# Moving both FFN layers ahead of the attention heads, rolling two engines' loops, and storing the output from 128 partitions

## Chip, cores and metric

One core of one Trainium2 chip. The metric is device microseconds (us) of one execution; lower is better. Every kernel was run beside the kernel before on the same chip. The sessions were on different chips, so kernels of different sessions are best compared by their ratios to the kernel before. The time is longer than the "span" of a profile, which goes from the first to the last instruction: about 2.4 us in the kernel before.

## The reference, cut to what matters

One decode step: a layer norm, attention of one query against a cache of 8192 keys for 2 x 32 heads, and a two-layer FFN on the same normalised x; all three are added.

```python
# bf16: x [2,1,512]  k_cache, v_cache [2,32,8192,128]  wq [512,4096]  wo [4096,512]
#       w1 [512,1792]  w2 [1792,512]
xn = _layernorm(x)
q  = (xn @ wq).reshape(B, Sq, H, Dh).transpose(0, 2, 1, 3)
p  = softmax(einsum("bhqd,bhkd->bhqk", q, k_cache) * Dh ** -0.5)
o  = einsum("bhqk,bhkd->bhqd", p, v_cache)
out = x + o.transpose(0, 2, 1, 3).reshape(B, Sq, H * Dh) @ wo \
        + relu(xn @ w1) @ w2
```

K and V are 268.4 MB of the 280.5 MB read. Wq and Wo are 4.19 MB each, W1 and W2 1.835 MB each, and the output is 2 KB.

## The kernel before

All large loads go through one queue, issued by the sync engine, in this order: Wq, then K and V tiles (two head pairs ahead), then W1, W2 and Wo:

```python
nc.sync.dma_start(vs[1][:], A_wq...)
def _(sp):
    load_k(0); load_k(1); load_v(0)
    for t in range(NP - 1):
        if t + R < NP:
            sp.wait_ge(pT, NG * (t + 1))      # the K buffer is free after its transposes
            load_k(t + R)
        sp.wait_ge(sW, t + 1)                 # the V buffer is free after its products
        load_v(t + 1)
    sp.dma_start(x8[:], A_x...)
    sp.dma_start(w1_sb[:], ...); sp.dma_start(w2_sb[:], ...)
    for c in range(3):                        # Wo in rows 0:16, 16:28, 28:32
        sp.dma_start(wo_sb[:, sl, :], wo_v[:, sl, :]).then_inc(dW[2 + c], 16)
    sp.wait_ge(sE, 1)
    sp.dma_start(out.rearrange("b s (c p) -> (b s c) p", p=P), osb[:]).then_inc(dO, 16)
```

For each of 32 head pairs, PE transposes a K tile in 16 groups of 8 (`transposes`), DVE and ACT copy the groups to SBUF (`kcopy`), PE multiplies them with q (`scores`) and then multiplies the previous pair's V tile (`weighted`). DVE and ACT are unrolled over the 32 pairs. The tail, after the last V tile:

```python
# PE
ffn(0, FT // 2); ... ; ffn(FT // 2, FT)       # W1 as weights, 56 matmuls of 2 columns
project(w2_sb, hT, 0, FT, first=True)         # W2 as weights, 56 matmuls
for c in range(3):
    pe.wait_ge(dW[2 + c], 16)
    project(wo_sb, OX, cuts[c], cuts[c + 1])  # lhsT = wo[:, j, c*128:(c+1)*128]
pe.wait_ge(sV, 105)
pe.transpose(tp[1][0:8, 0, :], yT)            # 128 x 8 -> 8 x 128
# DVE
v.tensor_tensor(out=yT[:], in0=ot[0]..., in1=xT..., op=ALU.add)
v.tensor_copy(osb[:], tp[1][0:8, 0, :])       # then the store: 8 rows of 256 B
```

Of the kernel before, what the change touches and what calls it, by code (L numbers as in the profile page):

```python
# [11 lines left out]
R = 2  # L12
# [7 lines left out]
def kernel(  # L20
# [31 lines left out]
    assert KT * H * Dh == SLOT  # L52
    inv_sqrt = float(Dh) ** -0.5
# [10 lines left out]
    def sem(name):  # L64
        return tc.alloc_semaphore(name)
# [4 lines left out]
    wo_sb = sb([P, WJ, D], bf16, "wo_sb")  # L70
    w1_sb = sb([P, KT, Dff], bf16, "w1_sb")
    w2_sb = sb([P, FT, D], bf16, "w2_sb")
    kT = [sb([P, EG, P], bf16, f"kT{i}") for i in range(4)]
    identb = sb([P, P], bf16, "identb")
    sel = sb([H, DQ, P], bf16, "sel")
# [4 lines left out]
    x8 = sb([Bsz * KT, P], bf16, "x8")  # L80
    xT = sb([P, Bsz * KT], f32, "xT")
# [5 lines left out]
    xnT = sb([P, KT, Bsz], bf16, "xnT")  # L87
# [8 lines left out]
    OTf = sb([P, N + 2], f32, "OTf")  # L96
# [4 lines left out]
    hT = sb([P, FT, Bsz], bf16, "hT")  # L101
    yT = sb([P, Bsz, KT], bf16, "yT")
    osb = sb([Bsz * KT, P], bf16, "osb")
# [15 lines left out]
    dX, dX8, dO = sem("dX"), sem("dX8"), sem("dO")  # L119
    dK = [sem(f"dK{i}") for i in range(R)]  # L120
    dV = [sem(f"dV{i}") for i in range(R)]
    dW = [sem(f"dW{i}") for i in range(5)]
    sG, sI, sQ, sQ1 = sem("sG"), sem("sI"), sem("sQ"), sem("sQ1")
    sV, sA, sE = sem("sV"), sem("sA"), sem("sE")
    pT, sS, sT, sB, sW = sem("pT"), sem("sS"), sem("sT"), sem("sB"), sem("sW")
    kR = [sem(f"kR{e}") for e in range(NG)]
    sM, sX, sP, sO = sem("sM"), sem("sX"), sem("sP"), sem("sO")
    sH, sF = sem("sH"), sem("sF")
# [5 lines left out]
    cuts = (0, 16, 28, WJ)  # L134
    qp = ot[1][:, 0:N].rearrange("p (h b) -> p h b", b=Bsz)
# [3 lines left out]
    tpy = tp[2][:].rearrange("p g k -> p (g k)")[:, 0:Bsz * KT]  # L139
    hp = ot[1][:, 0:FT * Bsz].rearrange("p (j b) -> p j b", b=Bsz)  # L140
# [7 lines left out]

    nc.sync.dma_start(vs[1][:], A_wq.rearrange("(p kt) n -> p (kt n)", kt=KT)).then_inc(dV[1], 16)  # L149
    nc.scalar.dma_start(xsb[:], A_x.flatten_outer_dims()).then_inc(dX, 16)  # L150

    block = nc.Block(no_gpsimd_drain=True)
    block.__enter__()

    @block.sync
    def _(sp):
        load_k(0)
        load_k(1)
        load_v(0)
        for t in range(NP - 1):  # L160
            if t + R < NP:
                sp.wait_ge(pT, NG * (t + 1))
                load_k(t + R)
            sp.wait_ge(sW, t + 1)
            load_v(t + 1)
        sp.dma_start(x8[:], A_x.rearrange("b s (c p) -> (b s c) p", p=P)).then_inc(dX8, 16)  # L166
        sp.dma_start(w1_sb[:], B_w1.rearrange("(p kt) f -> p kt f", kt=KT)).then_inc(dW[0], 16)  # L167
        sp.dma_start(w2_sb[:], B_w2.rearrange("(p j) n -> p j n", j=FT)).then_inc(dW[1], 16)  # L168
        for c in range(3):
            sl = slice(cuts[c], cuts[c + 1])  # L170
            sp.dma_start(wo_sb[:, sl, :], wo_v[:, sl, :]).then_inc(dW[2 + c], 16)  # L171
        sp.wait_ge(sE, 1)
        sp.dma_start(
            out.rearrange("b s (c p) -> (b s c) p", p=P), osb[:]
        ).then_inc(dO, 16)


    @block.gpsimd
    def _(g):
# [16 lines left out]
        for u in range(2):  # L196
            g.memset(onesh[u * HP:(u + 1) * HP, u, :], 1.0).then_inc(sI, 1)
            g.wait_ge(sI, 3 + u)
        g.wait_ge(sV, 100)
        for t in range(NP):  # L200
            if t >= R:
                g.wait_ge(sS, t - R + 1)
            g.tensor_copy(q2[t % R][:], qb[:, 2 * t:2 * t + 2]).then_inc(sQ1, 1)  # L203


    @block.tensor
    def _(pe):
# [6 lines left out]
        pe.wait_ge(dV[1], 16)  # L214
        wq_sb = vs[1][:].rearrange("p (kt n) -> p kt n", kt=KT)
        for h in range(H):
            for kt in range(KT):
                i = pe.matmul(  # L218
                    qp[:, h, :],
                    lhsT=wq_sb[:, kt, h * Dh:(h + 1) * Dh],  # L220
                    rhs=xnT[:, kt, :],
                    start=(kt == 0),
                    stop=(kt == KT - 1),
                )
        i.then_inc(sQ, 1)

# [3 lines left out]
        def transposes(r, e):  # L230
            for i in range(EG):
                kk = e * EG + i
                t = pe.transpose(tp[e % 4][:, i, :], ks[r][:, kk * Dh:(kk + 1) * Dh], identb[:])  # L233
            t.then_inc(pT, 1)
# [66 lines left out]
        values(1, NP + 1, 16 * (NP // R + 1))  # L301
        for e in range(NG):
            weighted(1, e)


        w1_v = w1_sb[:].rearrange("p kt (f j) -> p kt j f", j=FT)

        def ffn(j0, j1):
            for j in range(j0, j1):
                for kt in range(KT):  # L310
                    t = pe.matmul(
                        hp[:, j, :],
                        lhsT=w1_v[:, kt, j, :],
                        rhs=xnT[:, kt, :],
                        start=(kt == 0),
                        stop=(kt == KT - 1),
                    )
            return t


        pe.wait_ge(sO, NP + 2)
        pe.wait_ge(sI, 4)
        dbp = Sc[0][:, 0:N].rearrange("p (t u) -> p t u", u=2)
        pe.wait_ge(dX8, 16)
        pe.transpose(tpy, x8[:], identb[0:Bsz * KT, 0:Bsz * KT])
# [3 lines left out]
        pe.wait_ge(dW[0], 16)  # L329
        ffn(0, FT // 2)  # L330

        pe.wait_ge(sV, 102)
# [4 lines left out]
        ffn(FT // 2, FT).then_inc(sF, 1)  # L337
        pe.wait_ge(sV, 103)
# [11 lines left out]

        fin = ot[0][:, 0:KT * Bsz].rearrange("p (b c) -> p c b", c=KT)

        def project(w, act, j0, j1, first=False, last=False):
            for j in range(j0, j1):
                for c in range(KT):
                    t = pe.matmul(  # L356
                        fin[:, c, :],
                        lhsT=w[:, j, c * P:(c + 1) * P],
                        rhs=act[:, j, :],
                        start=(first and j == j0 and c == 0),  # L360
                        stop=(last and j == j1 - 1 and c == KT - 1),
                    )
            return t

        pe.wait_ge(sF, 2)
        pe.wait_ge(dW[1], 16)
        project(w2_sb, hT, 0, FT, first=True)
        pe.wait_ge(sV, 104)
        for c in range(3):
            pe.wait_ge(dW[2 + c], 16)  # L370
            t = project(wo_sb, OX, cuts[c], cuts[c + 1], last=(c == 2))
        t.then_inc(sH, 1)
        pe.wait_ge(sV, 105)
        pe.transpose(
            tp[1][0:Bsz * KT, 0, :], yT[:].rearrange("p b c -> p (b c)"), identb[:]
        ).then_inc(sH, 1)
# [6 lines left out]
    @block.vector  # L383
    def _(v):
        v.memset(eps_t[:], eps).then_inc(sV, 1)
        v.memset(onesb[:], 1.0)
        v.memset(prm[R - 1][:], 0.0).then_inc(sP, 1)
# [17 lines left out]
        v.tensor_copy(xnT[:], tpx).then_inc(sV, 1)  # L405
# [3 lines left out]
            out=qb[:].rearrange("p (b h) -> p b h", b=Bsz),  # L409
            in0=qp.rearrange("p h b -> p b h"),  # L410
            scalar1=inv_sqrt,
            scalar2=None,
            op0=ALU.mult,
        ).then_inc(sV, 94)

        for t in range(NP):
            i = t % R
            for e in range(NG):
                if e not in ON_ACT:
                    v.wait_ge(pT, NG * t + e + 1)  # L420
                    kcopy(v, e)
            v.wait_ge(sS, t + 1)
# [6 lines left out]
            v.wait_ge(sT, t + 1)  # L429
# [4 lines left out]

        v.wait_ge(sH, 1)
        v.tensor_copy(xT[:], tpy)  # L436
        v.reciprocal(out=RD[:], in_=Sc[0][:, 0:N]).then_inc(sV, 1)
        v.wait_ge(sV, 101)
        v.tensor_tensor(
            out=OTn[:].rearrange("p b h -> p (b h)"), in0=OTf[:, 0:N], in1=RD[:], op=ALU.mult  # L440
# [3 lines left out]
        v.wait_ge(sF, 1)  # L444
        v.tensor_scalar(
            out=hT[:], in0=hp, scalar1=0.0, scalar2=None, op0=ALU.max,
        ).then_inc(sF, 1)
# [5 lines left out]
        v.tensor_tensor(  # L453
            out=yT[:],
            in0=ot[0][:, 0:KT * Bsz].rearrange("p (b c) -> p b c", c=KT),
            in1=xT[:].rearrange("p (b c) -> p b c", c=KT),
            op=ALU.add,
        ).then_inc(sV, 1)
        v.wait_ge(sH, 5)
        v.tensor_copy(osb[:], tp[1][0:Bsz * KT, 0, :]).then_inc(sE, 1)  # L460


    @block.scalar
    def _(a):
# [5 lines left out]
        def out_copy(t):  # L470
            c = 2 * t if t >= 0 else N
            a.wait_ge(sW, t + 2)
            a.copy(OTf[:, c:c + 2], ot[t % R][:, 0:2]).then_inc(sO, 1)  # L473

        a.copy(OTf[:, N:N + 1], eps_t[:]).then_inc(sO, 1)
        for t in range(NP):
            i = t % R
            for e in range(NG):
                if e in ON_ACT:
                    a.wait_ge(pT, NG * t + e + 1)  # L480
                    kcopy(a, e)
            a.wait_ge(sB, t + 1)
            a.copy(nm[i][:], bc_of(i)).then_inc(sA, 1)  # L483
            a.wait_ge(sA, t + 2)
            for u in range(2):
# [7 lines left out]
                    accum_out=RS[half, t:t + 1],  # L493
                )
            x.then_inc(sP, 1)
            out_copy(t - 1)
        out_copy(NP - 1)

    block.__exit__(None, None, None)
    nc.sync.wait_ge(dO, 16)  # L500
# [28 lines left out]
```

## Time and profile before

| | before |
|---|---|
| time, median of 6 runs (range) | 662.73 us (662.54 to 662.95) |
| span of the profiled run | 660.4 us |
| PE / DVE / ACT busy | 83% / 38% / 36% |
| read from HBM | 280.50 MB, one queue, 98.9% of the span |
| issue of the store to the end of the span | 660.4 - 657.63 = 2.8 us |

Read it from the transfers: the queue is busy in every slice (90% or more in all but the last, by the page's DMA row), and the landing events of the packed trace come in the order of the issues, 9.7 us apart for most of the 4.19 MB tiles. So an engine's busy share matters only where it delays an issue, or after the last byte. The prediction below shows those lines.

### The profile page before, as it was taken

How to read it: one execution, taken by the hardware profiler on the slowest of the kernel's cores; microseconds unless marked ns; L12 is line 12 of the kernel's file. 1: busy time of each engine (PE TensorE's matmuls, PEld its weight loads, DVE VectorE, ACT ScalarE, POOL GpSimd, SP SyncE). 2: the span in 40 equal slices, each digit the busy share in tenths (PEclk: the TensorE clock that was granted, in tenths of full speed). 3: DMA queues.
4: the chain of work that ended last, by engine and by line, in shares of the span. 5: the costliest groups of instructions: out<-in, count | busy, mean ns of one | idle time of the engine just before them, and what ended most of it. 6: DMA issues, size and time to landing. Idle time of an engine off the chain costs nothing.

```text
span 660.4 us, 26876 instructions
## 1 busy us (share of the span) xinstructions
PE 551.0 (83%) x12864; PEld 537.0 (81%) x12864; DVE 251.4 (38%) x433; ACT 236.7 (36%) x389; POOL 8.5 (1%) x44
## 2 busy tenths in 40 slices
PE   2577999898887889788798987887997878987976
PEld 2577999888887889788798887887987878987875
DVE  1233544344343434434344443343443433443411
ACT  1242444343433334333243343333343333343410
POOL 1000000000000000000000000000000000000000
PEclk9999999998898999889899898899898989997985
DMA  9999999999999999999999999999999999999995
GB/s 381 416 438 429 424 439 427 437 427 431 437 429 437 427 431 433 429 437 429 431 435 427 439 429 431 435 427 439 427 431 433 429 439 425 435 433 429 437 417 246
DMA packets 10133, 280.73 MB, mean 425 GB/s; under 512 B 1154, under 2 KB 1156, under 8 KB 1284
## 3 DMA queue, kind: packets, MB, share of 16 engines
q1 hardware_dynamic: 10112, 280.50, 98.9%
q8 instruction: 10, 0.16, 0.1%
q14 instruction: 7, 0.06, 0.0%
q10 hardware_dynamic: 4, 0.00, 0.0%
HBM read 280.50 MB, written 0.00 MB: 425 GB/s over the span
## 4 chain that ended last, share of the span: by engine, by line
DMA 62%; PE 34%; ACT 1%; issue 1%; SPq 0%; DVE 0%
DMA ks<-in_A_k_cache_dram 56%; PE tp L233 21%; PE Sc L240 10%; DMA wo_sb<-in_A_wo_dram 5%; PE ot L253 3%; ACT kT L380 1%; PE ot L356 0%; PE Sc L288 0%; PE Sc L291 0%; SPq L171 0%; SPq L168 0%; SPq L166 0%; SPq L149 0%; SPq L167 0%; SPq L147 0%
## 5 line engine op out<-in xcount | busy, mean ns | idle before, releaser
L233 PE MATMUL tp<-identb,ks 128*128 128x128 bf16 x4096 | 324.9, 229 | 77.8 <-DMA ks<-in_A_k_cache_dram 75.9
L380 DVE COPY kT<-tp 128x1024 bf16<-128x1024 bf16 x320 | 219.7, 691 | 332.9 <-PE tp L233 332.7
L233 PEld LDWEIGHTS tp<-identb,ks 128*128 128x128 bf16 x4096 | 256.1, 103 | 81.3 <-DMA ks<-in_A_k_cache_dram 79.1
L380 ACT COPY kT<-tp 128x1024 bf16<-128x1024 bf16 x192 | 194.3, 1012 | 249.6 <-PE tp L233 249.6
L240 PE MATMUL Sc<-q,kT 128*128 128x64 bf16 x4096 | 216.3, 196 | 3.4 <-ACT kT L380 3.4
L240 PEld LDWEIGHTS Sc<-q,kT 128*128 128x128 bf16 x4096 | 178.4, 100 | 6.7 <-ACT kT L380 6.7
L253 PE MATMUL ot<-prm,vs 128*128 128x64 bf16 x4224 | 157.6, 193 | 8.5 <-issue 5.0
L253 PEld LDWEIGHTS ot<-prm,vs 128*128 128x128 bf16 x4224 | 140.5, 98 | 11.4 <-issue 8.8
L483 ACT COPY nm<-Sc 128x2 f32<-128x2 f32 x32 | 5.1, 160 | 118.2 <-PE Sc L291 118.2
L487 ACT ACTIVATE prm<-Sc,nm 64x128 bf16<-64x128 f32 x64 | 25.8, 402 | 1.4
L425 DVE TENSOR_REDUCE mcol<-Sc 64x1 bf16<-64x128 f32 x64 | 18.6, 291 | 17.6 <-PE Sc L240 17.2
L473 ACT COPY OTf<-ot 128x2 f32<-128x2 f32 x33 | 5.3, 160 | 35.3 <-PE ot L253 35.3
L430 DVE TENSOR_REDUCE mx<-Sc 1x2 bf16<-1x128 bf16 x32 | 8.9, 279 | 16.9 <-PE Sc L288 16.9
L203 POOL COPY q<-qb 128x2 bf16<-128x2 bf16 x32 | 5.8, 184 | 582.3 <-PE Sc L240 568.6
L487 ACT ACTIVATION_READ_ACCUMULATOR prm<-Sc,nm 64x1 f32 x64 | 11.8, 185 | 0.0
L218 PE MATMUL ot<-xnT,vs 128*128 128x2 bf16 x128 | 3.6, 165 | 8.3 <-DMA vs<-in_A_wq_dram 8.3
L218 PEld LDWEIGHTS ot<-xnT,vs 128*128 128x128 bf16 x128 | 3.5, 104 | 8.4 <-issue 8.4
L288 PE MATMUL Sc<-identb,mcol 128*1 128x128 bf16 x32 | 7.0, 217 | 0.0
L356 PE MATMUL ot<-OX,wo_sb 128*128 128x2 bf16 x128 | 3.7, 166 | 3.1 <-DMA wo_sb<-in_A_wo_dram 3.1
L356 PEld LDWEIGHTS ot<-OX,wo_sb 128*128 128x128 bf16 x128 | 3.6, 104 | 3.3 <-DMA wo_sb<-in_A_wo_dram 1.9
L291 PE MATMUL Sc<-mx,onesb 1*128 1x2 bf16 x32 | 5.5, 172 | 0.0
L436 DVE CAST xT<-tp 128x8 f32<-128x8 bf16 x1 | 0.2, 166 | 12.5 <-PE Sc L327 12.5
(49 smaller groups left out, 29.4 us busy)
## 6 DMA issues: line engine op xcount, KB each, us to landing
ks<-in_A_k_cache_dram SPq DMA_DIRECT2D x32, 4096.0 KB, 26.8
vs<-in_A_v_cache_dram SPq DMA_DIRECT2D x32, 4096.0 KB, 31.6
vs<-in_A_wq_dram SPq DMA_DIRECT2D x1, 4096.0 KB, 12.2
w_sb<-in_B_w_dram SPq DMA_DIRECT2D x2, 1792.0 KB, 25.9
wo_sb<-in_A_wo_dram SPq DMA_DIRECT2D x1, 2048.0 KB, 32.3
wo_sb<-in_A_wo_dram SPq DMA_DIRECT2D x1, 1536.0 KB, 35.5
wo_sb<-in_A_wo_dram SPq DMA_DIRECT2D x1, 512.0 KB, 36.3
xsb<-in_A_x_dram ACTq DMA_DIRECT2D x1, 2.0 KB
```

The lines of the kernel that those rows point to most:

```text
L203: g.tensor_copy(q2[t % R][:], qb[:, 2 * t:2 * t + 2]).then_inc(sQ1, 1)
L218: i = pe.matmul(qp[:, h, :], lhsT=wq_sb[:, kt, h * Dh:(h + 1) * Dh], rhs=xnT[:, kt, :], start=(kt == 0), stop=(kt == KT - 1),)
L233: t = pe.transpose(tp[e % 4][:, i, :], ks[r][:, kk * Dh:(kk + 1) * Dh], identb[:])
L240: t = pe.matmul(Sc[r][:, 2 * kk:2 * kk + 2 * REP], lhsT=kT[e % 4][:, i, :], rhs=rep(q2[r][:]), start=True, stop=True,)
L253: t = pe.matmul(ot[r][:, 0:2 * REP], lhsT=vs[r][:, kk * Dh:(kk + 1) * Dh], rhs=rep(prm[r][:, kk, :]), start=(kk == 0), stop=(kk == KB - 1),)
L288: pe.transpose(tr_of(r), mcol[r][:], identb[:]).then_inc(sT, 1)
L291: pe.matmul(bc_of(r), lhsT=onesb[:], rhs=mx[r][:], start=True, stop=True).then_inc(sB, 1)
L356: t = pe.matmul(fin[:, c, :], lhsT=w[:, j, c * P:(c + 1) * P], rhs=act[:, j, :], start=(first and j == j0 and c == 0), stop=(last and j == ...
L380: fn(kT[e % 4][:], tp[e % 4][:]).then_inc(kR[e], 1)
L425: m = v.tensor_reduce(out=mcol[i][half, :], in_=S_of(i)[half, :, u], axis=AX.X, op=ALU.max)
L430: v.tensor_reduce(out=mx[i][:], in_=tr_of(i).rearrange("o (u m) -> o u m", u=2), axis=AX.X, op=ALU.max, negate=True,).then_inc(sX, 1)
L487: x = a.activation(out=prm[i][half, :, u], in_=S_of(i)[half, :, u], func=ACTF.Exp, bias=nm[i][half, u:u + 1], scale=1.0, accum_out=RS[half ...
```

## The change

The intent: take the FFN out of the tail, so that only Wo follows the last V; shrink the instruction streams of DVE and ACT with loops; and drop the transpose and the copy between the last sum and the store, by letting each partition hold 4 neighbouring output columns and storing them as they lie. The core of the diff:

```diff
+    nc.sync.dma_start(w1_sb, B_w1...)                   # ahead of Wq
     nc.sync.dma_start(vs[1][:], A_wq...)
+        sp.dma_start(w2_sb, B_w2...)                    # ahead of the first K
         load_k(0)
...
-        sp.dma_start(x8...); sp.dma_start(w1_sb...); sp.dma_start(w2_sb...)
+        for i in range(2):                              # last V tile in two halves
+            sp.dma_start(vs[(NP - 1) % R][:, sl], V_all[(NP - 1) * P:NP * P, sl])
-    cuts = (0, 16, 28, WJ)
+    cuts = (0, 14, 21, 27, 30, WJ)
-            out.rearrange("b s (c p) -> (b s c) p", p=P), osb[:]
+            out.rearrange("b s (p c) -> p (b s) c", c=KT), yT[:]
...
+    # front, PE: FFN layer one and q now have x as weights and W1, Wq as moving data
+                pe.matmul(hp..., lhsT=xz[:, kt, ...], rhs=w1_v[:, kt, 4*g:4*g+nj, :])   # 16, step 28 B
+                pe.matmul(qp, lhsT=xz[:, kt, ...], rhs=vs[1][:, ...512 columns])        # 32
+    # small transposes of both, then layer two
+                pe.matmul(y, lhsT=hT[...], rhs=w2_sb[:, j, :])                          # 14
+    # DVE: ys = y + x, [2, 512] in float32
...
+    # tail, PE: ys into the accumulator as columns, then V, then Wo at a step of 8 B
+        ys_v = ys[:].rearrange("b (p k) -> b k p", k=KT)
+        wo_c = wo_sb.rearrange("p j (c k) -> p j k c", k=KT)
+            pe.matmul(fin[:, k, :], lhsT=ys_v[:, k, :], rhs=ident2[:], ...)             # 8 passes
-        pe.transpose(tp[1][0:Bsz * KT, 0, :], yT...)
-        v.tensor_copy(osb[:], tp[1][0:Bsz * KT, 0, :])
+        v.tensor_copy(yT[:], ot[0]...)                   # then the store, 256 runs of 8 B
...
-        for t in range(NP):                              # DVE and ACT, unrolled
+        with v.Fori(0, NP // R): ...                     # and the same on ACT
-    nc.sync.wait_ge(dO, 16)                              # who waits for the store
+        g.wait_ge(dO, 16); g.nop()
```

## The prediction

The prediction's sum was 0 - 0.9 + 0.6 - 0.1 = -0.4 us, or 662.4 us. Taken out, at the marked places, are statements that no trace or run of this case shows: a ceiling for the rate of the stream, a size rule for small transfers, the reason for taking 29 ns a product at a step of 8 bytes (and with it the argument against rival B), and the cost of a branch. The author's estimate: the 29 ns, which is what the contiguous Wo weights took, and the -0.1 for the instructions. That the stream can't be fed faster than the 431 to 432 GB/s of the stretch table was not shown. The 0.6 for the short runs was an estimate too, with no such store in the trace of before. "Cold" and "warm" stand for two rates of K's transposes in that trace, 0.89 ns a column in the first 24 (2.74 us) and 0.44 later (the weight loads of a group of 8 took 0.46 us); the granted clock was 1.00 in both stretches (24.3 to 27.0 and 28 to 34 us), and what makes the first ones slower was not shown.

> **What bounds the kernel now.** I read the page's slices first, then the stretch table (busy time, granted clock, DMA share and GB/s of each stretch), then the waits, then the order of time at the end.
>
> The page's DMA row and rate row:
>
> ```profile
> DMA  9999999999999999999999999999999999999995
> GB/s 381 416 438 429 424 439 427 437 427 431 437 429 437 427 431 433 429 437 429 431 435 427 439 429 431 435 427 439 427 431 433 429 439 425 435 433 429 437 417 246
> HBM read 280.50 MB, written 0.00 MB: 425 GB/s over the span
> ```
>
> Every slice but the last is full. The rate is flat near 431 GB/s. The stretch table says the same with its last two columns (DMA share, GB/s); the first figures are PE, PEld, DVE, ACT and POOL busy, then the clock:
>
> ```profile
> 128.00:256.00 128.00, 109.01 (x2508) 106.22 (x2504) 51.15 (x85) 48.03 (x78) 1.11 (x6) 0.95 1.00 432
> 384.00:512.00 128.00, 110.30 (x2513) 107.93 (x2514) 51.48 (x86) 48.82 (x77) 1.10 (x6) 0.93 1.00 432
> 650.00:657.00 7.00, 3.71 (x128) 3.57 (x128) 0.13 (x1) 0.00 (x0) 0.00 (x0) 0.50 0.52 214
> ```
>
> PE is 85% busy there, DVE 40%, ACT 38%; the queues are at 1.00. The waits view shows who has slack:
>
> ```profile
> PE tp L233 <- DMA ks<-in_A_k_cache_dram: 75.9, 27, 7.4
> PE Sc L240 <- ACT kT L380: 3.4, 16, 0.2
> SPq L173 <- DVE osb L460: 37.3, 1, 37.3
> ```
>
> PE waits for a K tile in 27 steps, 2.8 us each, and for the copies on ACT almost never. So the bound is the byte stream: 280.5 MB through one queue, first in first out. Only three things can move the time: the bytes, a gap in the stream, and what follows its last byte.
>
> The order of time at the end shows what follows it (start, length, engine, line):
>
> ```profile
> 637.79 5.53 PE L253 MATMUL ot<-prm,vs 128*128 128x64 bf16 x128 [3.50 <-DMA vs<-in_A_v_cache_dram]
> 644.14 1.80 PE L311 MATMUL ot<-xnT,w_sb 128*128 128x2 bf16 x28
> 651.28 1.85 PE L356 MATMUL ot<-OX,wo_sb 128*128 128x2 bf16 x64 [1.31 <-DMA wo_sb<-in_A_wo_dram]
> 656.87 0.17 DVE L453 TENSOR_TENSOR yT<-ot,xT 128x8 bf16<-128x8 f32 x1 [8.25 <-PE ot L356]
> 657.09 0.27 PE L374 MATMUL tp<-identb,yT 128*8 128x128 bf16 x1 [0.26 <-DVE yT L453]
> 657.39 0.21 DVE L460 COPY osb<-tp 8x128 bf16<-8x128 bf16 x1 [0.36 <-PE tp L374]
> 657.63 0.32 SPq L173 DMA_DIRECT2D out_dram<-osb  x1
> ```
>
> The last V tile is usable at 637.8. After it the queue carries W1, W2 (1.835 MB each) and Wo (4.194 MB), 7.86 MB, which at 430 GB/s takes 18.3 us and ends at 656.1. That agrees with the DMA view: the last Wo piece, issued about 619.9, has 36.3 us to landing, which is 656.2. The FFN (from 644.1) lies wholly beside these transfers. Behind the last byte come the last piece's matmuls to 656.8, the add, a transpose, a copy, the issue at 657.6 and the store to 660.4: 4.2 us, 0.6% of the kernel. The measured 662.76 is the span plus 2.3 us.
>
> [...] The new store has 256 runs of 8 B; no transfer of the kernel before is like it, so its cost is open. [...] W1's weights, taken at a step of 14 bf16 (28 bytes), come 1.80/28 = 64 ns apart, Wo's contiguous ones 1.85/64 = 29 ns. The new Wo view steps 4 bf16, 8 bytes,[...] so I take it as 29 ns. [...]
>
> **Part by part.**
>
> *FFN weights ahead.* Bytes removed: none (only the 2 KB second copy of x). W1 and W2, 3.67 MB, move from behind the last V to ahead of the first K, so every K and V arrives 3.67/0.43 = 8.5 us later (the first K usable at about 32.8 instead of 24.3), and Wo still ends at about 656.1. Transfer part: 0.
>
> *New work at the front.* W1 can be used at about 3.5 + 4.3 = 7.8 us (3.5 is Wq's 13.3 less the 9.75 us of its 4.19 MB), Wq at about 18, W2 at about 22, the first K at about 33. The FFN's first layer has 16 matmuls, 12 of 512 and 4 of 256 columns, 7168 in all; q has 32 of 512, 16384 in all. For the rate I take the first 24 transposes of K: 24 of 128 columns in 2.74 us, 0.89 ns a column, while later groups of 8 take 0.45 us, 0.44 ns a column. So the first layer takes 3 to 6 us and is done before Wq is there. q takes 7 to 15 us, done at 25 to 33. Its copy and two sets of small transposes add 1 us, and layer two, 14 matmuls of 512, adds 3 to 6. PE is ready for K at about 31 (warm) to 40 (cold throughout). The stream doesn't care unless a K issue is late. In the kernel before, the third K is issued at 36.5, which is 12.3 us after the first K could be used, and the queue would have run dry at 24.3 + 2 x 9.75 = 43.8. That 7.3 us of slack stands with everything 8.5 us later, and PE's lag of 0 to 7 us eats into it. Expected: 0; in the cold case up to 2 us.
>
> *Rolled DVE and ACT.* The work is the same, plus a branch and two register adds per two pairs[...], beside PE's 2.8 us of slack in each step. Instruction bytes shrink by less than the 0.22 MB that the two instruction queues carry in all. Expected: 0, at best -0.2 us.
>
> *Last V in halves, Wo in pieces of 14, 7, 6, 3 and 2 rows.* V's last half lands at about 646.3. Behind it on PE and DVE: 64 matmuls, 2.3 us (half of the 5.53); the product 0.2; transposes 0.4; copy 0.3; four selection matmuls 0.4; cast 0.2; waits between, about 0.5. That is 4.3 us, to 650.6, when Wo's first 14 rows land too (14/32 of 9.75 us after V). The pieces then come at 652.7, 654.5, 655.4 and 656.1, and PE needs 28, 24, 12 and 8 matmuls of 29 ns for them, 0.8 us or less each. It keeps up. After the last byte 8 matmuls remain: 0.25 us and some 0.1 us of wait, to 656.4 instead of 656.82. Gain 0.4 us.
>
> *Store.* Removed: transpose and second copy, that is issue at 657.63 less the end of the add at 657.04, 0.6 us, less about 0.05 for the issue's own wait. So the issue moves from 657.63 to about 656.7, 0.9 us earlier in all. Added: 16 short writes on each of 16 DMA engines in place of one row on each of 8. My estimate is 0 to 1.5 us, 0.6 in the middle, set against the 2.8 us that the present store takes from issue to the end of the span.
>
> Sum: 0 (transfer) - 0.9 (earlier issue) + 0.6 (short runs) - 0.1 (instructions) = -0.4 us, or 662.4 us.
>
> **Rivals.**
>
> *A. The move pays.* If the 7.86 MB behind the last V were an exposed tail, taking the 3.67 MB out would save 8.5 us (654). For it: the store's queue waits 37.3 us there, and the chain of waits calls Wo the last wait. Against it: the queue is full from start to end, and the same bytes pass earlier. I give it 2%.
>
> *B. Strided Wo weights become the end.* If a step of 8 bytes costs the 64 ns of the 28-byte step, the 128 matmuls take 8.2 us from 650.6, to 658.8, after the last byte: 2.4 us later than my 656.4, so about 665. For it: the only strided row in the trace is slow.[...] I give it 20%.
>
> *C. A new gap in the stream.* A cold PE at the front, or rolled loops that slow the copies between transposes and scores, make K issues late. ACT's copies are already in the chain now and then (1.02 us each), but PE waits only 3.4 us for them in all. It would show as a slice under 420 GB/s and cost 1 to 4 us: 664 to 667. I give it 10%.
>
> *D. The store's short runs cost more* than the transpose saved, 2 us or more: 664. I give it 15%.
>
> **Range and chances.** Everything that the change removes beside the stream is 1 us, and the rivals B to D add 1 to 4 us each. The eight-in-ten range is 660.9 to 664.6. Two per cent is 13 us; only a large gap in the stream or rival A far beyond its size would reach it. Faster by over 2%: 1%. Within 2%: 97%. Slower by over 2%: 2%.
>
> **What would show it right or wrong.** Right: 280.5 MB still read; a flat rate near 431 GB/s; first K transpose at 31 to 40 us; the last Wo matmul within 0.5 us of the last Wo landing; Wo matmuls 29 ns apart; a store issued about 0.9 us before where it was relative to the last landing. B is right if the Wo matmuls stand 64 ns apart and DMA ends first; C if a slice before the last is under 420 GB/s with PE or the issuing queue waiting; D if the span ends over 3.5 us after the store's issue. The prediction fails as a whole if the last byte of Wo lands more than 2 us from 656.

## The result, and the profile after

| | before | after |
|---|---|---|
| time, median of 6 runs each (range) | 662.73 (662.54 to 662.95) | 664.12 (663.39 to 664.80) |
| ratio (95%) | | 1.0021 (1.0008 to 1.0034) |
| span of the profiled run | 660.4 | 661.3 |
| issue of the store | 657.63 | 656.75 |
| issue to the end of the span | 2.8 | 4.5 |

A ratio is the mean time of one kernel's runs over that of the other's of the same rounds, so it is not quite the ratio of the medians quoted. The change is 1.4 us slower by the medians. The profiled run of after was its fastest (663.39), so its trace shows the smaller part of that: the median span of its six runs is 662.1, not 661.3.

The stream of the kernel after, from the page: the DMA share, the rate and the total.

```profile
DMA  8999999999999999999999999999999999999995
GB/s 365 442 422 431 433 432 432 426 434 434 430 434 426 438 428 430 436 432 432 430 428 440 428 430 434 428 438 428 428 436 434 430 430 428 440 428 430 434 421 212
HBM read 280.50 MB, written 0.00 MB: 424 GB/s over the span
```

The same bytes at the same flat rate: moving 3.67 MB from the end of the queue to its front cost nothing that shows in the transfers (the landing events of the packed traces put Wo's last piece at 655.53, before it was 656.16). The waits of the kernel after (total, times, longest) say the same of PE:

```profile
PE tp L297 <- DMA ks<-in_A_k_cache_dram: 67.9, 26, 3.4
PE Sc L304 <- ACT kT L423: 5.6, 15, 1.4
```

PE still waits for K, 2.6 us in each of 26 steps (67.9/26).

The end of the span after, in order of time (start, length):

```profile
643.87 0.60 PE L372 MATMUL Sc<-RS,onesh 128*128 128x32 f32 x4 [0.38 <-issue]
644.40 2.02 PE L378 MATMUL ot<-ident,ys 2*128 2x2 f32 x8
646.36 4.23 PE L317 MATMUL ot<-prm,vs 128*128 128x64 bf16 x128
652.10 4.42 PE L412 MATMUL ot<-OX,w_sb 128*128 128x2 bf16 x128 [0.32 <-DVE OX L511]
656.56 0.17 DVE L515 CAST yT<-ot 128x8 bf16<-128x8 f32 x1 [4.52 <-PE ot L412]
656.75 0.40 SPq L193 DMA_DIRECT2D out_dram<-yT  x1
```

No bracket names a DMA any more: V's 128 products and Wo's 128 follow one another without waiting for data. In the kernel before, both had waited for theirs. The store is issued 0.88 us earlier than before. But of this store the view of the transfers (bytes, us from issue to landing) and the waits of the sync engine's queue say:

```profile
out_dram<-yT SPq DMA_DIRECT2D x1, 2.0 KB, 3.2
```

```profile
SPq L193 <- DVE yT L515: 30.8, 1, 30.8
SPq L60 <- POOLq L60: 2.2, 1, 2.2
```

It lands 3.2 us after its issue, and the last line is the sync engine at the end of the program, waiting 2.2 us for POOL, which waits for the landing. (A transfer "lands" when the last of its completion events comes.)

### The profile page after: what moved, and what is told of

The parts are those of the page before. It is cut to its first block, busy times and chain, and to the rows that moved or that the text cites. A ratio compares the mean times of both kernels' runs of the same rounds, so it can differ in the third digit from the quotient of the medians.

```text
span 661.3 us, 26785 instructions
## 1 busy us (share of the span) xinstructions
PE 567.3 (86%) x12700; PEld 535.7 (81%) x12700; DVE 253.4 (38%) x436; ACT 255.8 (39%) x403; POOL 9.0 (1%) x46
## 3 DMA queue, kind: packets, MB, share of 16 engines
q1 hardware_dynamic: 10784, 280.50, 98.8%
HBM read 280.50 MB, written 0.00 MB: 424 GB/s over the span
## 4 chain that ended last, share of the span: by engine, by line
DMA 54%; PE 41%; ACT 2%; issue 1%; DVE 0%; ACTq 0%; SPq 0%
DMA ks<-in_A_k_cache_dram 53%; PE tp L297 21%; PE Sc L304 11%; PE ot L317 4%; PE ot L248 2%; ACT kT L423 2%; PE ot L259 1%; DMA w_sb<-in_B_w_dram 1%; PE ot L412 1%; PE Sc L282 0%; ACT L423 0%; PE ot L378 0%; PE Sc L352 0%; DVE qs L457 0%; PE Sc L355 0%
## 5 line engine op out<-in xcount | busy, mean ns | idle before, releaser
L297 PE MATMUL tp<-identb,ks 128*128 128x128 bf16 x4096 | 324.6, 229 | 70.3 <-DMA ks<-in_A_k_cache_dram 67.9
L317 PEld LDWEIGHTS ot<-prm,vs 128*128 128x128 bf16 x4224 | 139.0, 97 | 4.0 <-issue 1.3
L423 ACT ACT_TABLE_LOAD x16 | 20.5, 1283 | 2.2
L248 PE MATMUL ot<-w_sb,xz 128*8 128x512 bf16 (+1 forms) x16 | 12.9, 975 | 3.9 <-DMA w_sb<-in_B_w_dram 3.9
L528 ACT COPY OTf<-ot 128x2 f32 x32 | 5.1, 160 | 22.4 <-PE ot L317 22.4
L248 PEld LDWEIGHTS ot<-w_sb,xz 128*8 128x8 bf16 x16 | 1.6, 103 | 14.3 <-issue 14.3
L540 ACT ACTIVATION_READ_ACCUMULATOR prm<-Sc,nm x64 | 11.8, 185 | 0.0
L259 PE MATMUL ot<-vs,xz 128*16 128x512 bf16 x32 | 8.0, 415 | 0.0
L259 PEld LDWEIGHTS ot<-vs,xz 128*16 128x16 bf16 x32 | 3.1, 97 | 5.2 <-issue 2.1
```

What stands on the lines that cost most here:

```text
L248: i = pe.matmul(hp[:, 0:nj * P].rearrange("c (l f) -> c l f", f=P), lhsT=xz[:, kt, Z - g * Bsz:Z - g * Bsz + FG * Bsz], rhs=w1_v[:, kt, 4 ...
L259: i = pe.matmul(qp, lhsT=xz[:, kt, Z - g * Bsz:Z - g * Bsz + QG * Bsz], rhs=vs[1][:, (kt * QG + g) * 512:(kt * QG + g + 1) * 512], start=( ...
L297: t = pe.transpose(tp[e % 4][:, i, :], ks[r][:, kk * Dh:(kk + 1) * Dh], identb[:])
L317: t = pe.matmul(ot[r][:, 0:2 * REP], lhsT=vs[r][:, kk * Dh:(kk + 1) * Dh], rhs=rep(prm[r][:, kk, :]), start=(kk == 0), stop=(kk == KB - 1),)
L423: fn(kT[e % 4][:], tp[e % 4][:]).then_inc(kR[e], 1)
L540: x = a.activation(out=prm[i][half, :, u], in_=S_of(i)[half, :, u], func=ACTF.Exp, bias=nm[i][half, u:u + 1], scale=1.0, accum_out=RS[half ...
```

## The experiments

My theory after the result: the 256 runs of 8 bytes make the store land later than 8 rows do, by more than the removed transpose and copy were worth. The rivals: POOL's wait or the changed end of the program costs it, not the store; the tail of PE costs it (strided Wo, float32 products, or the clock); the rolled ACT and DVE cost it; or the slower front does. Twelve kernels tell them apart. Below, "issue to end" is the end of the span less the start of the store's issue. Where a landing is quoted, it is that of the transfers' view.

**The change again (a0), and the wait for the store on SP instead of POOL (b).**

> The changed kernel again, as the yardstick of this call. All theories: within the 663.4 to 664.8 us of its six runs, 0.1 to 0.3% slower than before.

```diff
-        g.wait_ge(dO, 16); g.nop()
+        sp.wait_ge(dO, 16)          # after the store
```

> Changed kernel, but the last store is waited for on SP, as before, not on POOL. Theory store (the 8-byte runs themselves take 3.2 us from issue to landing): no change, within 0.2 us of the changed kernel, span still ends 4.4 to 4.6 us after the store's issue. Rival POOL (the waiting engine wakes up late or tears down more slowly): 1 to 1.5 us faster than the changed kernel, span ends about 3 us after the issue.

a0: 663.78 us, ratio 1.0020 (1.0006 to 1.0034); landing 3.3, issue to end 4.8. It repeats the result in another set of runs. b: 665.39, ratio 1.0032 (1.0018 to 1.0046), landing 3.2, issue to end 5.2. The landing doesn't change with the engine that waits, and the end doesn't come sooner, so POOL's wait is not the cause. That b would stay within 0.2 us of a0 failed. b's profiled run is slower than after's because its store is issued at 658.01. The stretch table shows why, here for the V products (after first, then b; the last three columns are PE's clock, the DMA share and GB/s):

```profile
646.30:650.60 4.30, 4.28 (x129) 4.06 (x129) 0.00 (x0) 0.00 (x0) 0.00 (x0) 1.00 0.97 399
```

```profile
646.30:650.60 4.30, 4.30 (x94) 4.30 (x94) 0.00 (x0) 0.00 (x0) 0.00 (x0) 0.60 0.97 401
```

In the same 4.3 us b's PE was granted 0.60 of its clock and did 94 products instead of 129. The spans of b's five runs are 661.4 to 663.4, those of a0's 661.1 to 662.7: the tail falls in a slow or a fast stretch of the clock. Why b met slow ones more often, I can't show. It matters for reading all that follows: after, a0, b, j, q16 and q32 have the same tail up to the store, and their profiled runs issue it anywhere between 656.32 and 658.15, with a median of 657.5. After's own 656.75 is an early one.

**The same kernel, with the old store (c).** Contiguous Wo weights, transpose, copy, 8 rows of 256 bytes; everything else as after.

```diff
-            out.rearrange("b s (p c) -> p (b s) c", c=KT), yT[:]
+            out.rearrange("b s (c p) -> (b s c) p", p=P), osb[:]
-        ys_v = ys...("b (p k) -> b k p");  wo_c = wo_sb...("p j (c k) -> p j k c")
+        ys_v = ys...("b (k p) -> b k p");  wo_c = wo_sb...("p j (k c) -> p j k c")
+        pe.transpose(tp[1][0:Bsz * KT, 0, :], yT...)
+        v.tensor_copy(osb[:], tp[1][0:Bsz * KT, 0, :])
```

> Changed kernel with the old store: Wo weights contiguous, transpose into 8 rows, store of 8 rows. Theory store: the Wo matmuls go from 34.5 to 29 ns apart (0.7 us less, or less than that where the last piece of Wo is waited for), the issue comes 0.55 us later after the add, the landing takes 1.4 us less; sum 1 to 1.6 us faster than the changed kernel, so equal to before or up to 0.5 us better. Rival stream (FFN ahead or rolled loops slow the stream): no faster than the changed kernel, or 0.5 us slower for the transpose.

661.93 us (661.45 to 662.18), ratio 0.9985 (0.9971 to 0.9998): 1.85 us under a0 (1 to 1.6 had been expected), and under the kernel before. Its end, from the order of time:

```profile
653.13 3.57 PE L413 MATMUL ot<-OX,w_sb 128*128 128x2 bf16 x128 [0.32 <-DVE OX L516]
657.51 0.37 SPq L194 DMA_DIRECT2D out_dram<-osb  x1
```

The issue is 0.76 us later than after's, and yet the span ends at 660.1, 1.2 us earlier: 2.6 us after the issue instead of 4.5. So the old form of the store is worth 1.9 us after the issue. The Wo products take 3.57/128 = 28 ns each instead of 34.5, which is 0.85 us in all.

**The kernel before, with the new store (f).** The strided Wo and W2 weights and the store of 8-byte runs (and x turned into columns by four small transposes to match); the FFN stays behind the heads and nothing is rolled.

```diff
-            out.rearrange("b s (c p) -> (b s c) p", p=P), osb[:]
+            out.rearrange("b s (p c) -> p (b s) c", c=KT), yT[:]
-                        lhsT=w[:, j, c * P:(c + 1) * P],
+                        lhsT=w[:, j, :].rearrange("p (q k) -> p k q", k=KT)[:, c, :],
-        pe.transpose(tp[1]..., yT...);  v.tensor_copy(osb[:], ...)
```

> Kernel before with the new store alone (residual by four strided transposes of x, Wo weights at a step of 8 bytes, 8-byte runs). Theory store: last Wo matmul 0.3 us later, issue 0.55 us earlier after the add, landing 1.4 us later: 0.9 to 1.3 us slower than before, nearly all of what the whole change loses. Rival stream: within 0.3 us of before.

665.48 us, ratio 1.0042 (1.0028 to 1.0056). The new store with what feeds it makes the kernel before slower, by 2.7 us, where 0.9 to 1.3 had been expected. In both kernels the sync engine itself waits for the store, so this row of its waits can be compared, before first, then f:

```profile
SPq L56 <- DMA out_dram<-osb: 0.4, 1, 0.4
```

```profile
SPq L56 <- DMA out_dram<-yT: 3.7, 1, 3.7
```

The wait grows by 3.3 us, while the issue comes only 0.24 us earlier (657.39): the Wo products, at 2.30/64 = 36 ns, give back most of what the transpose saved. f's landing is 4.6 us, not 3.2. I have no experiment for the further 1.4, and it stays open.

**The FFN part alone (k).** c with DVE and ACT unrolled again, so only the FFN, the halves of V and the pieces of Wo are left of the change.

```diff
-        with v.Fori(0, NP // R): ... pair(r, reg)
+        for t in range(NP):
+            pair(t % R, t + 1)            # the same on ACT
```

> FFN ahead alone: old store and unrolled DVE and ACT. Theory (rolling lies beside the stream; the 16 added table loads of 1.28 us on ACT are in its slack): within 0.4 us of the rolled kernel with the old store, 661.9 us. Rival (rolling costs on the path): 0.5 to 1.5 us faster than that.

661.79 us, ratio 0.9984 (0.9971 to 0.9997), against c's 0.9985. Rolling shows no gain or loss that these runs can tell (each ratio is known to 0.13%), though it is not free on ACT. The groups of the kernel after show what it does (busy time, mean ns of one, idle time before):

```profile
L423 ACT ACT_TABLE_LOAD x16 | 20.5, 1283 | 2.2
```

Sixteen loads of the activation table, one in each round of the loop, 1.28 us each. k and the kernel before have two loads in all. That they cost nothing visible is what k against c shows; the likely reason is that 1.28 us a round is less than PE's wait for K in a step, 2.6 us.

**Taking work out of PE's tail, two ways (e, g; m1, m2).** If the tail of PE were what costs, taking 2 us out of it would help. e moves the 8 float32 products of `ys` from the tail to the front; g is e with c's store.

```diff
+        # before the head loop
+        pe.matmul(fin[:, k, :], lhsT=ys_v[:, k, :], rhs=ident2[:], ...);  pe.wait_ge(sF, 8)
-        # in the tail: the same 8 products
-        v.tensor_copy(yT[:], ot[0]...)
+        v.tensor_tensor(out=yT[:], in0=ot[0]..., in1=ysT[:], op=ALU.add)
```

> Changed kernel, with the eight fp32 products that turn the FFN result plus x into columns (2.0 us on PE in the tail) moved ahead of the heads; the last DVE step adds instead of copying. Theory PE tail (since the change, PE runs without a wait from the last K tile's landing to the last Wo matmul and sets the end): the store is issued 0.8 to 1.5 us earlier, as far as the landing of Wo's last piece, near 655.5 us, allows; median 662.3 to 663.0 us, and less spread than the changed kernel's 1.5 us. Rival (Wo's transfers set the end, PE has slack): no change, within 0.2 us. The landing of the store stays near 3.2 us under both.

> FFN ahead and rolled loops, with the old store of 8 rows and the column products moved ahead. Theory PE tail plus store: the last Wo piece's landing sets the end again; span 659.0 to 659.6, median 660.8 to 661.6 us, spread under 0.6 us, 0.2 to 0.3% faster than before. Rival (only the store mattered): no faster than the changed kernel with the old store, 661.9 us.

e: 665.59 us (663.81 to 666.58), ratio 1.0033 (1.0018 to 1.0047), no faster than after and 1.5 us slower by the medians, though the intervals overlap. g: 662.26 (661.60 to 663.85), ratio 0.9989 (0.9976 to 1.0002), no better than c. Both expectations failed. A new loss is at the other end of the kernel. In e the first K transposes start at 37.56 instead of 33.39, and the third K is issued so late that the queue runs dry; in the order of time of the queue, after first, then e:

```profile
44.33 0.33 SPq L162 DMA_DIRECT2D ks<-in_A_k_cache_dram  x1
```

```profile
49.69 0.33 SPq L163 DMA_DIRECT2D ks<-in_A_k_cache_dram  x1
```

The stretches 50 to 55 and 70 to 75 of after, then of e, with the rate last:

```profile
50.00:55.00 5.00, 2.67 (x52) 2.49 (x49) 0.69 (x1) 1.37 (x4) 0.00 (x0) 0.90 0.98 416
70.00:75.00 5.00, 3.64 (x92) 3.39 (x88) 1.29 (x2) 3.52 (x8) 0.00 (x0) 1.00 0.99 423
```

```profile
50.00:55.00 5.00, 4.24 (x126) 3.96 (x123) 1.25 (x4) 0.95 (x5) 0.18 (x1) 1.00 0.91 347
70.00:75.00 5.00, 4.71 (x135) 4.41 (x132) 2.09 (x5) 0.76 (x4) 0.18 (x1) 1.00 0.87 315
```

Over the first 100 us the rate is 410 GB/s instead of 421, which is 1.1 MB or about 2.6 us of stream lost, and it never comes back: the last K can be used at 628.19 instead of 626.14. So e is no test of the tail. It shows where the front's slack ends: with the third K issued at 44.33 (after) the stream is whole, with 49.69 it is not.

m1 therefore takes the work out without loading the front: layer one, q and layer two with the weights stationary as in the kernel before (two columns moving), `ys` already in columns, one add at the end. m1 has the new store, m2 the old one.

```diff
-        rhs=w1_v[:, kt, 4 * g:4 * g + nj, :]  (16 matmuls of 512 or 256 columns)
+        lhsT=w1_v[:, kt, j, :], rhs=xnT[:, kt, :]   (56 matmuls of 2; q 128; layer two 56)
-        8 products of ys in the tail
+        v.tensor_tensor(out=yT[:], in0=ot[0]..., in1=ysT[:], op=ALU.add)
```

> Changed kernel, with its front computed as the kernel before computes it (weights stationary, two columns moving, results already in columns: 56 + 128 + 56 matmuls, 3.6 + 3.6 + 1.9 us by the rows of before), so that the column products leave the tail without making PE late for the first K tile. New store kept. Theory PE tail: PE waits for the first K again (third K issued at about 45 us or earlier, no stretch of the stream under 400 GB/s after 30 us), Wo's products end 1 to 2 us earlier than in the changed kernel, as far as Wo's landing near 655.5 allows; median 662.3 to 663.2 us. Rival (the tail is set by Wo's landing): as the changed kernel, 663.8 to 664.1 us.

> The same front with the old store of 8 rows. Theory PE tail plus store: median 660.8 to 661.7 us, the best of all, 0.15 to 0.3% under before. Rival: as the changed kernel with the old store, 661.9 us.

m1: 664.19 us (663.87 to 664.31), ratio 1.0017 (1.0003 to 1.0030). m2: 662.38 (661.99 to 662.49), ratio 0.9989 (0.9975 to 1.0003). The front becomes much shorter. In the order of time, layer one after, then in m1:

```profile
8.55 12.92 PE L248 MATMUL ot<-w_sb,xz 128*8 128x512 bf16 x16 [3.92 <-DMA w_sb<-in_B_w_dram]
```

```profile
8.58 3.49 PE L239 MATMUL ot<-xnT,w_sb 128*128 128x2 bf16 x56 [2.58 <-DMA w_sb<-in_B_w_dram]
```

The stream is whole with this too: m1's third K is issued at 45.59, after's at 44.33. At the end the tail of PE is now early enough that it waits for Wo again (the waits of m1 between 618 and 662 us):

```profile
PE ot L375 <- DMA w_sb<-in_A_wo_dram: 2.2, 3, 0.9
```

And m1 is not faster than after: its store is issued at 657.02. I had expected some 1 us from the shorter tail, and this failed, and m2's 660.8 to 661.7 with it. Two ends are nearly tied here, the last piece of Wo and the chain of PE; taking one away leaves the other. (m1's spans, 661.6 to 661.8, are no longer than a0's median of 661.8, but its time outside the span is about 2.5 us instead of 2.0; why stays open.) What m1 does change is the spread: 0.44 us over five runs, where after has 1.41 over six. m1 and m2 differ in the store and what feeds it alone: m1 issues 0.66 us earlier (657.02 against 657.68) and ends 1.4 us later (661.7 against 660.3). Issue to end is 4.7 and 2.6.

**Two stores of half the run length (j).** Output columns 0:2, then 2:4: 512 runs of 4 bytes.

```diff
-        sp.dma_start(out..., yT[:]).then_inc(dO, 16)
+        for q in range(2):
+            sp.dma_start(out_v[:, :, 2*q:2*q+2], yT[:, :, 2*q:2*q+2]).then_inc(dO2[q], 16)
```

> Changed kernel with the store split into two stores of 4-byte runs, 512 runs in all. Theory per run (each short run costs time in the landing): the second store lands 4.5 us or more after the first issue, of which 0.4 is its own later issue, and the kernel is 1 to 2 us slower. Theory fixed (a short-run store pays one fixed delay, whatever its runs): second landing 3.6 to 3.8 us after the first issue, kernel 0.4 to 0.6 us slower.

668.70 us (668.50 to 668.96), ratio 1.0083 (1.0069 to 1.0098), by the ratios some 4 us slower than a0, where 1 to 2 had been expected. The tile view of the output in j:

```profile
DMA to landing us min/median/max: 3.1/4.8/6.6
```

The first store lands as after's does, and the second 6.6 us after its own issue. Issue to end is 666.7 - 658.15 = 8.5 us. A delay that overlapped for the two stores is ruled out. A fixed delay for each store, paid one after the other, is not: by the packed trace the first completion event of the second store (662.96) comes after the last of the first (661.24). The next two kernels decide that, with one store each.

**Fewer, longer runs (q16, q32).** The same 2 KB from 64 partitions in runs of 16 bytes (128 runs), or from 32 in runs of 32 (64 runs). The stored data are zeros, so the result is wrong; all other work, and the wait of the store for it, stay. "Theory fixed" is j's: one fixed delay for a store of short runs.

```diff
-            out.rearrange("b s (p c) -> p (b s) c", c=KT), yT[:]
+            out.rearrange("b s (p c) -> p (b s) c", c=8), zz[:]      # q32: c=16
```

> Changed kernel that stores the same 2 KB of zeros from 64 partitions in 128 runs of 16 bytes (the result is wrong on purpose; everything before the store is unchanged). Theory per run (landing grows with the number of short runs, (3.2 - 1.3)/248 = 7.7 ns each between 8 runs and 256): landing 2.2 to 2.4 us, kernel 0.8 to 1.0 us faster than the changed kernel. Theory fixed[...]: landing near 3.2 us, no change.

> The same from 32 partitions in 64 runs of 32 bytes (result wrong on purpose). Theory per run: landing 1.7 to 1.9 us, kernel 1.3 to 1.5 us faster than the changed kernel. Theory fixed: landing near 3.2 us, no change.

q16: 662.60 us, ratio 1.0000 (0.9983 to 1.0017). q32: 663.18, ratio 1.0007 (0.9991 to 1.0024). The kernel times are not in the order of the landings, since q32's tail of PE ran late and its store was issued at 658.11, q16's at 657.06. The landings themselves, q16 first, then q32:

```profile
DMA to landing us min/median/max: 1.9/1.9/1.9
```

```profile
DMA to landing us min/median/max: 1.5/1.5/1.5
```

In the table, "packets over" is the end of the store's last packet record after the issue. These records, and the completion events that give the landing of the 8 rows, are in the packed traces (`trace.npz`); no view prints them.

| store | kernels | packets over us | landing us | issue to end us |
|---|---|---|---|---|
| 8 rows of 256 B | before, c, g, k, m2 | 0.9 | 1.2 | 2.8, 2.6, 2.6, 2.7, 2.6 |
| 64 runs of 32 B | q32 | 1.0 | 1.5 | 3.0 |
| 128 runs of 16 B | q16 | 1.6 | 1.9 | 3.3 |
| 256 runs of 8 B | after, a0, e, m1 | 1.2 | 3.2, 3.3, 3.3, 3.3 | 4.5, 4.8, 4.7, 4.7 |
| 256 runs of 8 B, waited for by SP | b, f | 1.2 | 3.2, 4.6 | 5.2, 6.4 |
| 2 x 256 runs of 4 B | j | 1.7 (both) | second: 6.6 | 8.5 |

All these stores move 2 KB. Sending the packets is not what takes long: after's 256 are over 0.25 us after the first starts (256 packets of 8 B and 16 of 4 B, where the store of before has 8 of 256 B and 8 of 4 B). The time lies between the last packet and the last completion: 0.3 to 0.5 us with 8 rows and with runs of 32 or 16 bytes, 2.0 to 2.2 us with 256 runs of 8 (f: 3.4). After's 16 completion events come one by one between 1.5 and 3.2 us after the issue. So the delay doesn't rise evenly with the number of runs, and the 7.7 ns a run expected before q16 failed: q16 lands later than q32 only because its first packet starts 1.37 us after the issue instead of 0.84. The step lies between 128 runs of 16 bytes and 256 of 8. Whether the count of runs, their length or the number of partitions makes it, these kernels can't separate, since one sets the others; and what goes on after the last packet, no record shows.

## Why the prediction was right or wrong

The predicted time, 662.4 us, is 1.7 below the measured 664.12, and the sign was wrong: slower by 0.2% instead of faster by 0.05%. The range (660.9 to 664.6) and the class, within 2%, hold. Two steps failed: what ends the tail before the store (PE, not the transfers), and the size of the short runs. By its own steps:

- **The transfer part, 0: right.** 280.50 MB both times, a flat rate, and the moved bytes worth nothing; Wo's last piece lands at 655.53, for 656.1 predicted. Rival A is out.
- **The front, cost 0: right in the sum, wrong inside.** Layer one was put at 3 to 6 us and took 12.92, as the groups of the kernel after show (busy time, mean ns of one; matmuls overlap, 12 x 1088 ns being 13.1 us where 11.1 were busy, so the spacing is the busy time over the count):

```profile
L248 PE MATMUL ot<-w_sb,xz 128*8 128x512 bf16 x12 | 11.1, 1088 | 3.9 <-DMA w_sb<-in_B_w_dram 3.9
L259 PE MATMUL ot<-vs,xz 128*16 128x512 bf16 x32 | 8.0, 415 | 0.0
```

  W1 as moving data at a step of 28 bytes stands 11.1/12 = 0.92 us apart for 512 columns, Wq's contiguous columns 8.0/32 = 0.25 us. The granted clock was 1.00 in both stretches. That layer one is PE's first long work doesn't explain it: its first four matmuls (8 to 12 us) average 1084 ns, its last four of 512 columns (16 to 20 us) 1091. No run changes the step alone, though. q's 8.03 us are inside the predicted 7 to 15. PE was ready for K at 33.39, inside the predicted 31 to 40 and 1.3 us after the first K had landed (32.12, by the landing events). Rival C did not happen here. e shows how near it was: with K's transposes 4 us later the stream has its gap. The slack of 7.3 us was overstated too. By that working the queue would run dry at 43.8 + 8.5 = 52.3, and e's third K, issued 2.6 us ahead of that, was already too late. The likely reason is that the working counted from when tiles can be used, which is later than when the queue has moved most of them: the 16 completion events of the first K spread over 1.8 us in the trace of before (22.44 to 24.23).
- **Rolled loops, 0 to -0.2: right**, with a cost that the step had not named. Sixteen table loads, 20.5 us of ACT, with no cost in the time that k against c could show. The two instruction queues carried 0.14 MB, where they had carried 0.22. The cost of a branch by itself, no run here shows.
- **V's halves and 64 products after the last one: failed.** The prediction let V's last half be what PE waits for. From the last K at 626.14 on, PE waited for no transfer; the chain ran through PE (with one ACT copy of 1.0 us and waits of 0.3 to 0.4 us for DVE in it): the step of the last pair up to 643.5, then 0.6 us of row sums, 2.02 us of `ys` products that the prediction left out, and all 128 V products from 646.36 on, after both halves had landed (640.71 and 645.60). Wo's products began at 652.10, not 650.6. In their place the step should have been a chain of PE from the last K on. The halves of V bought nothing in this run.
- **The last Wo product at 656.4: right by compensation.** It ended at 656.52, though by PE and not by the last byte: 1.0 us after Wo's last landing, where the prediction's own mark was 0.5. This chain also hangs on the granted clock, which is the likely source of the spread of 1.4 us (b's stretch at 0.60 points to it; m1, whose end waits for Wo, hasn't the spread). The typical run of after is some 0.7 us slower than its profiled one; that its late runs are late in this stretch was not profiled.
- **Wo at 29 ns a product: half right.** 34.5 ns at the step of 8 bytes, against 28 in c: 0.85 us for 128. The clock doesn't explain it (granted 0.80 in after, 0.50 in c), and f's 36 ns against 29 in the kernel before were both at 0.50. Rival B's 64 ns is refuted.
- **The store 0.9 us earlier: right in the profiled run, not in the typical one.** 657.63 to 656.75 there; but the six profiled runs with this tail issue it at 657.5 in the median, 0.1 us earlier than before. And relative to Wo's last landing, which was the prediction's mark, the profiled run gains 0.25 us (1.47 to 1.22). So the number 0.9 was met by luck of the clock; the chain of PE had taken most of the gain.
- **The short runs, +0.6 us: the mis-sized term.** From issue to end 2.8 us became 4.5, so it is +1.8 by before and after, +1.9 by c and after, and +2.1 by m1 and m2. The mechanism was in the sum and as rival D, whose mark (over 3.5 us from issue to end) it met; its size was outside the 0 to 1.5 that I allowed.

In the profiled runs -0.9 + 1.8 = +0.9 us is the difference of the spans, by construction. For the typical run it is about -0.1 + 1.8 = +1.7, and the median span of after's six runs, 662.1, is indeed 1.7 above 660.4. The times differ by less, 1.4, because after spends 0.3 us less outside its span.

Where did the hoped-for gain go? The FFN had been hidden beside the transfers before (644.14 to 649.97, with Wo's last piece landing at 656.16), so moving it freed nothing on the path. c and k show what the rest was worth with the old store: 0.15%, about 1 us. Of that, 0.3 to 0.4 us lies outside the span (2.0 to 2.1 us against 2.4), so it is not in the tail at all; their profiled spans are shorter by 0.3 and 0.7 us, and which piece of the tail brings that, I did not separate. k, at 661.79 us, is the best version run here, and c is not to be told from it.

## What to carry to other kernels

Here the queue was full from start to end (98.9% of the span before, 98.8% after), and the order in it was worth nothing; in such a kernel ask instead what follows the last byte, and what the new order puts between the last tile and the end on the compute engine. The store that ended this program had no work to hide behind, so its form counted in full: a transpose and a copy of 0.6 us bought rows that landed 1.2 us after the issue, about 2 us sooner than 256 short runs (3.2). And before moving work to the front, work out how late the first refill may be issued; in e, what the queue lost past that point, about 2.6 us, never came back.
